# Two score matmuls on half the rows each: pairing the lower-part products of an attention tile on TensorE

## The chip, the core and the metric

One NeuronCore of one Trainium2 chip runs the whole program. The metric is the device time of one execution in microseconds (us): the median of several runs, and beside it the one execution that was taken with the hardware profiler, from which all rows come.

## What is computed

The program chains three blocks. The change is in the first, an attention with queries pooled by two:

```python
q_pool = q.reshape(B, H, S // 2, 2, D).mean(axis=3)      # B=2, H=8, S=1152, D=64
scores = scale * np.matmul(q_pool, k.transpose(0, 1, 3, 2))
scores = scores - np.max(scores, axis=-1, keepdims=True)
attn = np.exp(scores)
attn = attn / (np.sum(attn, axis=-1, keepdims=True) + 1e-09)
return np.matmul(attn, v)
```

The two blocks behind it are feed-forward layers: `x @ w_in`, a leaky ReLU, `@ w_out`; then four experts `relu(x @ w1[e]) @ w2[e]`, weighted by probabilities and added.

## The kernel before

**Two parts of every number.** Matmul operands are held as two parts, a higher one (`hi`, a copy into the matmul's type) and a lower one (`lo`, what is left over). A product is the sum of higher by higher, higher by lower and lower by higher.

**Pairs and tiles.** `pairs` lists 2 batches x 4 pairs of heads, `n` = 0 to 7. A pair has 9 tiles `t` of 128 query rows: `t` = 0 to 3 belong to its first head, 5 to 8 to its second, and `t` = 4 holds 64 rows of each. `tiles` lists all 72.

**Score operands.** `kst[n][h]`, called `K[h]`, has the head's keys on 128 partitions: the higher parts of the 64 dimensions on partitions 0 to 63, the lower parts on 64 to 127. `qst[n % 2][:, j, h]` has the queries, the same 64 dimensions on both halves of the partitions, with `j` = 1 for higher and `j` = 0 for lower parts (from pair 1 on). So one matmul with the higher parts of the queries gives two of the three products at once, and one with the lower parts gives the third (and the product of the two lower parts, which isn't needed). `kh_b[n % 2]`, called `k_hi_of[n]`, has the higher parts of both heads' keys: head 0 on partitions 0 to 63, head 1 on 64 to 127.

**The steps of one tile.** `emit_s` (L346) issues the scores, 1152 columns in three chunks of `CW` = 384, each in a PSUM bank of its own: per chunk a matmul with the queries' higher parts and one with their lower parts, so six matmuls a tile (nine for `t` = 4, of which three use `qmid`). VectorE (DVE) then moves the three banks to SBUF in one instruction and takes the minimum (L349); there is one set of three banks, so the next tile's scores wait for that. ScalarE (ACT) takes the exponential (L355), DVE adds 1e-9 and takes the reciprocal (L359, L363), GpSimd (POOL) normalises (L365). `emit_t` transposes the nine 128x128 blocks on TensorE (L386); ACT copies their higher parts (L390), DVE subtracts for the lower ones (L98, `tl`). `queue_av` lists the products with the values (L413) and `run_av` issues some of them in each tile.

**What sets the order.** The order is written out by hand: a loop over `tiles` emits, for tile `i`, the scores of tile `i + lead` (`lead` is 3 but for the first tiles), the transposes of tile `i`, some products with the values, the exponential of tile `i + lead`, and one step of the next pair's preparation from `prep_pair`. Its step `k_lo` has POOL take the keys' lower parts, and the SyncE (SP) queue copy higher and lower parts into `K[h]` (L282, L283); `q_lo` and its DMAs (L298) follow, and the loads of later pairs (L221, L222, L230). In the last pair DVE and ACT also prepare the first weights of the feed-forward block.

Of the kernel before, what the change touches and what calls it, by code (L numbers as in the profile page):

```python
# [27 lines left out]
CW = 384  # L28
# [5 lines left out]
def f32(ap):  # L34
    return ap.bitcast(F32)
# [3 lines left out]
def tile_kernel(ctx: ExitStack, tc: tile.TileContext, q, k, v, w_in, w_out, probs, w1, w2, out):  # L39
    nc = tc.nc  # L40
    PE, ACT, DVE, POOL, SP = nc.tensor, nc.scalar, nc.vector, nc.gpsimd, nc.sync

    def at(name, off, shape, dt=F32R):

        return nc.alloc_sbuf_tensor_at(name, [128, *shape], dt, offset=BASE + 4 * off).ap()
# [9 lines left out]
    qst = [at(f"qst{i}", 18432 + 2560 * i, [2, 2, SQ + 64]) for i in range(2)]  # L55
    qmid = [at(f"qmid{i}", 23552 + 128 * i, [128]) for i in range(2)]
    kh_b = [at(f"kh{i}", 23808 + 1152 * i, [S]) for i in range(2)]
    th_b = [at(f"th{i}", 26112 + 2880 * i, [NKB, 320]) for i in range(2)]
    tl_b = [at(f"tl{i}", 31872 + 2880 * i, [NKB, 320]) for i in range(3)]
    e_b = [at(f"e{i}", 41216 + 1152 * i, [S], F32) for i in range(5)]  # L60
# [28 lines left out]
    def hi(eng, dst, src):  # L89
        if eng is ACT:  # L90
            ACT.copy(dst, src)  # L91
        elif eng is POOL:
            POOL.tensor_scalar(dst, src, 1.0, 1.0, op0=ALU.mult, op1=ALU.mult)
        else:
            DVE.tensor_copy(dst, src)

    def lo(eng, dst, src, high):
        eng.tensor_tensor(dst, src, f32(high), op=ALU.subtract)  # L98
# [75 lines left out]
    def three_banks(i):  # L174
        return PS[:, 3 * i:3 * i + 3]
# [5 lines left out]
    def first_layer(f, src_h, src_l):  # L181
        ps = next_banks()
        wh, wl = a_t[f]

        def mms(k_, c):
            cs = slice(c * CW, (c + 1) * CW)
            PE.matmul(ps[:, c, :CW], wh[:, k_], src_h[:, k_, cs], start=k_ == 0, stop=False)  # L187
            PE.matmul(ps[:, c, :CW], wh[:, k_], src_l[:, k_, cs], start=False, stop=False)  # L188
            PE.matmul(ps[:, c, :CW], wl[:, k_], src_h[:, k_, cs], start=False, stop=k_ == KD - 1)  # L189
        return ps, mms  # L190


    with ExitStack() as actx:
# [15 lines left out]
        raw, raw_v, kst, vst, k_hi_of = {}, {}, {}, {}, {}  # L209

        def two_heads(n, name):
            return [kv[name, h, n % 2] for h in range(2)]

        def load_qk(n):
            if n >= len(pairs):
                load_a()
                load_a()
                return
            b, p = pairs[n]
            rk, rq = rk_b, rq_b.rearrange("p (a b) -> p a b", a=2)  # L220
            SP.dma_start(rk, k[b, p])  # L221
            SP.dma_start(rq, q[b, p])  # L222
            raw[n] = (rk, rq)

        def load_v(n):
            if n >= len(pairs):
                return
            b, p = pairs[n]
            raw_v[n] = rv_b.rearrange("p (a h d) -> p a h d", a=NKB, h=2)
            SP.dma_start(raw_v[n], v[b, p])  # L230
# [35 lines left out]
        def prep_pair(n):  # L266


            e_q, e_v = DVE if n == 1 else POOL, DVE if n == 0 else POOL
            rk, rq = raw.get(n, (None, None))  # L270

            def k_hi():
                kh = k_hi_of[n] = kh_b[n % 2]
                hi(ACT, kh, rk)

            def k_lo():
                kh = k_hi_of[n]
                ks = kst[n] = two_heads(n, "k")
                lo(POOL, rk.bitcast(F32R), rk, kh)
                for h in range(2):  # L280
                    r = slice(h * 64, h * 64 + 64)
                    SP.dma_start(f32(ks[h][0:64]), f32(kh[r]))  # L282
                    SP.dma_start(f32(ks[h][64:128]), rk[r])  # L283

            def q_add():
                POOL.tensor_tensor(rq[:, 0], rq[:, 0], rq[:, 1], op=ALU.add)

            def q_hi():
                hi(ACT, rq[:, 1].bitcast(F32R), rq[:, 0])

            def q_lo():
                lo(e_q, rq[:, 0].bitcast(F32R), rq[:, 0], rq[:, 1])
                t = qst[n % 2]
                for h in range(2):
                    r = slice(h * 64, h * 64 + 64)
                    hi(POOL, qmid[n % 2][r, r], rq[r, 0, (SQ - 64) * (1 - h):][:, :64])
                    for d in (slice(0, 64), slice(64, 128)):
                        SP.dma_start(f32(t[d, :, h, h * 64:h * 64 + SQ]), rq[r])  # L298

            def v_hi(h):  # L300
                if h == 0:
                    vst[n] = [t.rearrange("p (a b) -> p a b", a=NKB) for t in two_heads(n, "v")]
                a = h * 64
                hi(ACT, vst[n][h][:, :, a:a + 64], raw_v[n][:, :, h, :])

            def v_lo(h):
                a, c = h * 64, 64 - h * 64
                lo(e_v, vst[n][h][:, :, c:c + 64], raw_v[n][:, :, h, :], vst[n][h][:, :, a:a + 64])

            if n == 0:  # L310
                return [[lambda: v_hi(0)], [lambda: v_lo(0)], [lambda: v_hi(1)], [lambda: v_lo(1), lambda: load_v(1)]]
            return [[q_add, k_hi], [k_lo], [q_hi], [q_lo, lambda: load_qk(n + 1)], [lambda: v_hi(0)],
                    [lambda: v_lo(0), lambda: v_hi(1)], [lambda: v_lo(1), lambda: load_v(n + 1)]]
# [15 lines left out]
        def emit_s(i):  # L329
            n, t = tiles[i]  # L330
            ps = three_banks(0)
            Q, K = qst[n % 2], kst[n]
            if t < 4:
                use = [(0, t * 128)]
            elif t == 4:
                use = [(0, 512), (1, 0)]
            else:
                use = [(1, 128 + (t - 5) * 128)]
            for c in range(3):
                cs = slice(c * CW, (c + 1) * CW)  # L340
                mms = [(Q[:, j, h, c0:c0 + 128], K[h][:, cs]) for h, c0 in use for j in (1, 0)]
                if len(use) > 1 and n:

                    mms = mms[::2] + [(qmid[n % 2], k_hi_of[n][:, cs])]
                for m, (x, y) in enumerate(mms):
                    PE.matmul(ps[:, c, :CW], x, y, start=m == 0, stop=m == len(mms) - 1)  # L346
            e = e_b[i % 5].rearrange("p (a b) -> p a b", a=3)
            st = st_b[:, i % 6]
            DVE.tensor_scalar(e, ps[:, :, :CW], -0.5 / float(D) ** 0.5, None,  # L349
                              op0=ALU.mult, op1=ALU.min, accum_out=st[:, 0:1])  # L350
            s_sb[i] = (e, st)
# [89 lines left out]
        with tc.manual_schedule():  # L441
# [16 lines left out]
            at = dict.fromkeys(("s", "exp", "sum", "norm"), 0)  # L458

            def upto(what, emit, i):  # L460
                first = {"exp": "s", "sum": "exp", "norm": "sum"}
                while at[what] <= i and at[what] < (at[first[what]] if what in first else len(tiles)):
                    emit(at[what])
                    at[what] += 1

            upto("s", emit_s, 0)
            upto("exp", emit_exp, 0)
            q_lo(1)
            for c in range(3):
                k_hi(1, c)  # L470
            upto("s", emit_s, 1)
            upto("sum", emit_sum, 0)
            upto("norm", emit_norm, 0)
# [33 lines left out]
            for i, (n, t) in enumerate(tiles):  # L507
                if i in begin_at:
                    for d, fs in enumerate(prep_pair(begin_at[i])):
                        steps.setdefault(i + d, []).extend(fs)  # L510
                lead = 2 if i < L2 else 3
                upto("s", emit_s, i + lead)
                upto("sum", emit_sum, i + lead - 1)
                emit_t(i, lambda: upto("norm", emit_norm, i + lead - 1))
                run_av(AVB.get(t, AVD))
                if i == len(tiles) - 4:

                    f0_ps, mms = first_layer(0, xh, xl)
                    f0 = [(k_, c) for k_ in range(KD - 1) for c in range(NC)] + [(KD - 1, c) for c in range(NC)]
                if i >= len(tiles) - 4:  # L520
                    for _ in range(F0N[t - 5]):
                        mms(*f0.pop(0))
                upto("exp", emit_exp, i + lead)
                if t in (1, 4, 6, 8):
                    name, w = {1: ("A1", 256), 4: ("A2", 320), 6: ("B1", 320), 8: ("B2", 256)}[t]
                    queue_av(n, name, w, fast=n == len(pairs) - 1 and t > 4)
                for f in steps.get(i, []):
                    f()
                if n == len(pairs) - 1:
                    for f in ahead.get(t, []):  # L530
                        f()
# [207 lines left out]
    with tc.manual_schedule():  # L739
# [3 lines left out]
        ps, mms = first_layer(1, xh, xl)  # L743
# [8 lines left out]
        for f in range(2, n1):  # L752
            ps, mms = first_layer(f, xh, xl)
# [30 lines left out]
    with tc.manual_schedule():  # L784
# [24 lines left out]
        for what, *args in order:  # L809
            what(*args)  # L810
            if what is product:
# [5 lines left out]
                elif name == "P2" and p or name == "P7" and p == NPAIR - 1:  # L817


                    n = p - (name == "P2")  # L820
# [31 lines left out]
```

## Time and profile before

| | |
|---|---|
| median of 3 runs | 853.01 us (851.96 to 854.18) |
| the profiled execution | 852.96 us |
| its span, first to last instruction | 851.2 us |
| TensorE matmul (PE) busy | 824.2 us, 97% of the span |
| weight loads of TensorE (PEld) busy | 776.7 us, 91% |
| DVE / ACT / POOL busy | 574.0 / 435.4 / 412.6 us |
| mean granted TensorE clock | 0.990 |

The 1.8 us between the execution's time and its span lie before the first and behind the last instruction. Busy shares are means over stages that differ: attention fills the first 255 us or so, the feed-forward layers the rest. Matmuls are pipelined and the profile models their ends, so the duration of one matmul is longer than the distance from its start to that of the next.

### The profile page before, as it was taken

What the parts mean: (1) busy time and instruction counts of PE and PEld (TensorE: products, weight loads), DVE (VectorE), ACT (ScalarE), POOL (GpSimd) and SP (SyncE); (2) the same over time, 40 slices, a digit from 0 to 9 for tenths busy, and PEclk for the clock granted to TensorE, in tenths of its full rate; (3) what the DMA queues carried; (4) which work ended last, traced back from release to release, by engine and by line L of the source; (5) the groups of instructions that cost most, each with busy time, mean ns of one, the idle gap of its engine ahead of it and who ended that gap; (6) DMA issues with size and microseconds to landing.
All of it is one profiled execution on the core that took longest, in us unless ns stands there. A gap on an engine that the chain in (4) does not pass through costs nothing.

```text
span 851.2 us, 13547 instructions
## 1 busy us (share of the span) xinstructions
PE 824.2 (97%) x5071; PEld 776.7 (91%) x5071; DVE 574.0 (67%) x948; ACT 435.4 (51%) x763; POOL 412.6 (48%) x362
## 2 busy tenths in 40 slices
PE   6799999999989899999999999999999999999998
PEld 5689999999979799999999998989898998989886
DVE  5979999999997989777666772635445362726332
ACT  4878989999985665424422640505142342406030
POOL 1668888888862678565561060605133331504020
PEclk7999999999999999999999999999999999999999
DMA  7446446644701233322120020201111110201012
GB/s 195 111 127 181 106 132 169 157 105 131 197 5 63 85 111 111 99 71 78 51 99 25 26 99 1 99 1 53 47 50 50 49 51 1 99 1 50 0 38 99
DMA packets 25153, 68.65 MB, mean 81 GB/s; under 512 B 2944, under 2 KB 7040, under 8 KB 25088
## 3 DMA queue, kind: packets, MB, share of 16 engines
q1 hardware_dynamic: 25088, 67.79, 26.7%
q8 instruction: 40, 0.66, 0.3%
q14 instruction: 25, 0.20, 0.1%
HBM read 48.91 MB, written 2.36 MB: 60 GB/s over the span
## 4 chain that ended last, share of the span: by engine, by line
PE 82%; DVE 9%; issue 3%; DMA 2%; POOL 1%; ACT 1%; SPq 0%; POOLq 0%; DVEq 0%; ACTq 0%
PE ps L687 20%; PE ps L729 8%; PE ps L730 8%; PE ps L728 7%; PE ps L346 7%; PE ps L413 6%; PE ps L386 6%; PE ps L585 4%; PE ps L586 4%; PE ps L584 4%; DVE e L349 3%; PE ps L189 3%; PE ps L188 3%; PE ps L187 3%; DVE tl L98 2%
## 5 line engine op out<-in xcount | busy, mean ns | idle before, releaser
L98 POOL TENSOR_TENSOR bb<-w2r,bb 128x512 fp32r<-128x512 f32 x32 | 45.5, 1445 | 262.9 <-ACT bb L91 232.0
L735 DVE SCALAR_TENSOR_TENSOR oacc<-ps,pw,oacc 128x512 f32<-128x512 f32 x63 | 47.2, 749 | 101.4 <-PE ps L730 101.4
L365 POOL TENSOR_SCALAR e<-e,st 128x1152 f32<-128x1152 f32 x70 | 86.9, 1246 | 58.4 <-DVE st L363 42.4
L98 DVE TENSOR_TENSOR tl<-ps,th 128x384 fp32r<-128x384 f32 (+1 forms) x240 | 112.0, 503 | 1.9 <-ACT th L390 1.8
L729 PE MATMUL ps<-bb,gg 128*128 128x512 f32 x288 | 112.3, 390 | 0.9 <-POOL bb L98 0.8
L687 PE MATMUL ps<-yT,ws 128*128 128x288 f32 x768 | 111.5, 296 | 0.8 <-ACT cb L704 0.8
L728 PE MATMUL ps<-bb,gg 128*128 128x512 f32 x288 | 112.2, 390 | 0.0
L730 PE MATMUL ps<-bb,gg 128*128 128x512 f32 x288 | 112.1, 389 | 0.0
L349 DVE TENSOR_SCALAR_CACHE_REDUCE e<-ps 128x1152 f32<-128x1152 f32 x72 | 97.4, 1353 | 17.1 <-PE ps L346 16.1
L346 PE MATMUL ps<-k,qst 128*128 128x384 f32 x438 | 96.8, 353 | 11.8 <-DVE e L349 7.4
L687 PEld LDWEIGHTS ps<-yT,ws 128*128 128x128 f32 x768 | 105.7, 189 | 1.6 <-ACT cb L704 1.0
L390 ACT CAST th<-ps 128x384 fp32r<-128x384 f32 (+1 forms) x240 | 91.2, 458 | 25.1 <-PE ps L386 23.4
L693 ACT COPY ca<-ps 128x576 f32<-128x576 f32 x16 | 10.3, 641 | 167.6 <-PE ps L687 154.8
L355 ACT ACTIVATE e<-e,st 128x1152 f32<-128x1152 f32 x72 | 91.1, 1265 | 4.3 <-DVE e L349 2.6
L346 PEld LDWEIGHTS ps<-k,qst 128*128 128x128 f32 x438 | 77.0, 194 | 17.2 <-DVE e L349 11.7
L386 PE MATMUL ps<-ident,e 128*128 128x128 f32 x648 | 84.6, 276 | 4.9 <-POOL e L365 3.3
L386 PEld LDWEIGHTS ps<-ident,e 128*128 128x128 f32 x648 | 75.5, 142 | 10.6 <-POOL e L365 6.0
L687 PE MATMUL ps<-yB,ws 128*128 128x288 f32 x576 | 84.4, 296 | 0.0
L687 PEld LDWEIGHTS ps<-yB,ws 128*128 128x128 f32 x576 | 79.8, 189 | 0.5
L98 DVE TENSOR_TENSOR ws<-wf,ws 128x768 fp32r<-128x768 f32 (+1 forms) x32 | 41.5, 1298 | 46.3 <-ACT ws L91 46.3
L189 PE MATMUL ps<-xh,a 128*128 128x384 f32 x192 | 65.0, 339 | 2.8 <-POOL a L136 2.8
L187 PE MATMUL ps<-xh,a 128*128 128x384 f32 x192 | 64.9, 338 | 0.7 <-ACT gf L563 0.7
(126 smaller groups left out, 1723.7 us busy)
## 6 DMA issues: line engine op xcount, KB each, us to landing
wa<-in_w_in SPq DMA_DIRECT2D x16, 512.0 KB, 3.5
wb<-in_w_out SPq DMA_DIRECT2D x16, 512.0 KB, 4.2
wf<-in_w SPq DMA_DIRECT2D x32, 256.0 KB, 3.9
w2r<-in_w SPq DMA_DIRECT2D x16, 512.0 KB, 3.6
qst<-rq SPq DMA_DIRECT2D x28, 288.0 KB, 4.3
rv<-in_v SPq DMA_DIRECT2D x8, 576.0 KB, 5.5
rk<-in_k SPq DMA_DIRECT2D x7, 576.0 KB, 5.9
rq<-in_q SPq DMA_DIRECT2D x7, 576.0 KB, 4.8
```

The costliest lines, as they stand in the source:

```text
L98: eng.tensor_tensor(dst, src, f32(high), op=ALU.subtract)
L187: PE.matmul(ps[:, c, :CW], wh[:, k_], src_h[:, k_, cs], start=k_ == 0, stop=False)
L189: PE.matmul(ps[:, c, :CW], wl[:, k_], src_h[:, k_, cs], start=False, stop=k_ == KD - 1)
L346: PE.matmul(ps[:, c, :CW], x, y, start=m == 0, stop=m == len(mms) - 1)
L349: DVE.tensor_scalar(e, ps[:, :, :CW], -0.5 / float(D) ** 0.5, None, op0=ALU.mult, op1=ALU.min, accum_out=st[:, 0:1])
L355: ACT.activation(e, e, AF.Exp, bias=st[:, 0:1], scale=-1.0, accum_out=st[:, 1:2])
L386: PE.transpose(ps[:, j], e[:, (3 * g + j) * 128:(3 * g + j + 1) * 128], ident)
L390: ACT.copy(h, ps[:, :, s0:s0 + w])
L687: PE.matmul(ps[:, c, :HW], w[wi][:, i, ks], y[:, yi, k, c * HW:(c + 1) * HW], start=bool(first and k == 0 and m == 0), stop=k == 1 and m = ...
L728: PE.matmul(ps, gh[:, ts_], wh, start=f == fs[0], stop=False)
L729: PE.matmul(ps, gh[:, ts_], wl, start=False, stop=False)
L730: PE.matmul(ps, gl[:, ts_], wh, start=False, stop=f == fs[-1])
```

## The change

For every tile of pairs 1 to 7 but `t` = 4, the six score matmuls are written in another order and two of them on fewer rows. First come the three chunks with the queries' higher parts, on all 128 rows. Then chunk 2 with the lower parts, on 128 rows as before. Then chunk 0 with the lower parts on rows 0 to 63 alone (against the keys' higher parts there), and chunk 1 with the lower parts on rows 64 to 127 alone. For that the keys' higher parts of chunk 1 must lie on partitions 64 to 127. For the second head `k_hi_of[n]` has them there; for the first head one more DMA a pair copies 64 x 384 numbers into a new buffer `khs_b`. The product of the two lower parts is left out for chunks 0 and 1.

```diff
+    khs_b = [at(f"khs{i}", 51264 + CW * i, [CW]) for i in range(2)]
...
                     SP.dma_start(f32(ks[h][0:64]), f32(kh[r]))
                     SP.dma_start(f32(ks[h][64:128]), rk[r])
+                SP.dma_start(f32(khs_b[n % 2][64:128]), f32(kh[0:64, CW:2 * CW]))
...
-            for c in range(3):
+            if len(use) == 1 and n:
+                (h, c0), = use
+                hi_, lo_ = (Q[:, j, h, c0:c0 + 128] for j in (1, 0))
+                other = khs_b[n % 2] if h == 0 else k_hi_of[n][:, CW:2 * CW]
+                for c in range(3):
+                    PE.matmul(ps[:, c, :CW], hi_, K[h][:, c * CW:(c + 1) * CW], start=True, stop=False)
+                PE.matmul(ps[:, 2, :CW], lo_, K[h][:, 2 * CW:], start=False, stop=True)
+                PE.matmul(ps[:, 0, :CW], lo_[0:64], K[h][0:64, :CW], start=False, stop=True)
+                PE.matmul(ps[:, 1, :CW], lo_[64:128], other[64:128], start=False, stop=True)
+            for c in range(3) if len(use) > 1 or not n else ():
```

On TensorE's queue, at the first tiles of pair 1 (`k` is `K[0]`, `qst` the queries, `e` the normalised scores; 128x384 is what a matmul writes), there stood before:

```order
L346 MATMUL ps<-k_58,qst_66 128x384 x6
L386 MATMUL ps<-ident,e_77 128x128 x9
L413 MATMUL ps<-tl_74,v_61 128x320 x8
L346 MATMUL ps<-k_58,qst_66 128x384 x6
L386 MATMUL ps<-ident,e_78 128x128 x9
```

and now:

```order
L349 MATMUL ps<-k_58,qst_66 128x384 x3
L350 MATMUL ps<-k_58,qst_66 128x384
L351 MATMUL ps<-k_58,qst_66 128x384
L352 MATMUL ps<-khs_72,qst_66 128x384
L400 MATMUL ps<-ident,e_79 128x128 x9
L427 MATMUL ps<-tl_76,v_61 128x320 x8
L349 MATMUL ps<-k_58,qst_66 128x384 x3
L350 MATMUL ps<-k_58,qst_66 128x384
L351 MATMUL ps<-k_58,qst_66 128x384
L352 MATMUL ps<-khs_72,qst_66 128x384
L400 MATMUL ps<-ident,e_80 128x128 x9
```

The number of matmuls and their columns stay; the group is four matmuls on 128 rows, then the two on 64 rows (L351, L352), and the transposes come right behind these.

On SP's queue, at the preparation of pair 1 (`kh` the keys' higher parts of both heads, `rk` their lower parts), there stood before:

```order
L282 DMA k_58<-kh_70 64x1152
L283 DMA k_58<-rk 64x1152
L282 DMA k_60<-kh_70 64x1152
L283 DMA k_60<-rk 64x1152
L230 DMA rv<-in_v 128x1152
L298 DMA qst_66<-rq 64x2x576 x4
```

and now:

```order
L284 DMA k_58<-kh_70 64x1152
L285 DMA k_58<-rk 64x1152
L284 DMA k_60<-kh_70 64x1152
L285 DMA k_60<-rk 64x1152
L286 DMA khs_72<-kh_70 64x384
L232 DMA rv<-in_v 128x1152
L301 DMA qst_66<-rq 64x2x576 x4
```

One DMA is put between the copies of the keys and the next load of values; nothing else moves.

## Rows read from the trace of the kernel before

**Rows 1.** The page: engines (busy, share, instructions), then the span in 40 slices.

```profile
PE 824.2 (97%) x5071; PEld 776.7 (91%) x5071; DVE 574.0 (67%) x948; ACT 435.4 (51%) x763; POOL 412.6 (48%) x362
...
PE   6799999999989899999999999999999999999998
```

**Rows 2.** Busy time by stretch of 20 us, from 60 to 240 us, and their sum.

```profile
60.00:80.00 20.00, 19.34 (x141) 18.32 (x140) 18.56 (x49) 18.20 (x40) 18.89 (x20) 1.00 0.68 171
...
200.00:220.00 20.00, 19.90 (x149) 19.47 (x148) 19.20 (x50) 18.92 (x40) 17.72 (x18) 1.00 0.38 93
...
sum 180.00, PE 177.91 PEld 172.66 DVE 169.45 ACT 165.17 POOL 150.49; mean PE 19.77 PEld 19.18 DVE 18.83 ACT 18.35 POOL 16.72
```

**Rows 3.** The chain of waits over one pair: start us, us, what.

```profile
149.34 1.38 DVE e L349 x2
150.72 0.04 issue
150.76 1.31 PE ps L346 x6
152.07 0.98 PE ps L386 x9
153.06 1.19 PE ps L413 x10
154.25 1.05 PE ps L346 x6
...
173.60 1.07 PE ps L346 x6
...
178.50 1.36 DVE e L349
```

**Rows 4.** Groups of instructions from 149.3 to 178.5 us, the same pair.

```profile
L349 DVE TENSOR_SCALAR_CACHE_REDUCE e<-ps 128x1152 f32<-128x1152 f32 x9 | 12.2, 1353 | 1.4 <-PE ps L346 1.4
```

**Rows 5.** The chain of waits in the last pair: its tile `t` = 4, then the tail.

```profile
235.19 1.58 PE ps L346 x9
236.88 1.37 DVE e L349 x2
...
241.33 1.36 DVE e L349 x2
...
251.50 1.27 DVE e L349 x2
```

**Rows 6.** Line L346 alone in that pair: duration ns min/median/max.

```profile
L346 PEld LDWEIGHTS ps<-k,qst x54: 186/188/192, 150.8 to 177.7; 128*128 128x128 f32 x54
L346 PE MATMUL ps<-k,qst x54: 334/336/440, 150.8 to 177.9; 128*128 128x384 f32 x54
```

**Rows 7.** Timeline in mid tile, at 183.81 us: TensorE's matmuls, then its weight loads.

```profile
183.62 0.51 PE L346 MATMUL ps<-k,qst 128*128 128x384 f32 x2
...
183.62 0.36 PEld L346 LDWEIGHTS ps<-k,qst 128*128 128x128 f32 x2
```

**Rows 8.** Timeline at 179.9 us, a tile whose scores waited: matmul, then weight loads.

```profile
179.93 0.44 PE L346 MATMUL ps<-k,qst 128*128 128x384 f32 x1
...
179.92 0.30 PEld L346 LDWEIGHTS ps<-k,qst 128*128 128x128 f32 x2 [0.30 <-DVE e L349]
```

**Rows 9.** SP's queue over the preparation of pair 1, then its key copies' landing.

```profile
33.88 0.75 SPq L283 DMA_DIRECT2D k<-rk  x1
34.74 1.23 SPq L230 DMA_DIRECT2D rv<-in_v  x1
38.53 3.68 SPq L298 DMA_DIRECT2D qst<-rq  x4
...
k<-kh SPq DMA_DIRECT2D x14, 288.0 KB, 4.1
```

**Rows 10.** Waits ahead of the scores (us, times), then the chain at pair 1's start.

```profile
  DMA qst<-rq: 0.5, 1
...
43.02 0.60 issue
43.62 2.09 PE ps L346 x6
```

## The prediction

> **What bounds the kernel now.** I began with the page: PE is busy 97% of the span, and from the third slice on it shows 9 or 8 tenths throughout [rows 1]. That alone says little, since a matmul's duration is longer than its share of the queue. So I looked at the stage of the change by stretches of 20 us: between 60 and 240 us PE is busy 177.91 of 180 us, but DVE 169.45 (94%) and ACT 165.17 (92%) [rows 2]. The stage has little air anywhere. The chain of waits says who sets the pace: over one pair, from 149.34 to 178.50 us (29.16 us), it runs through scores (L346), transposes (L386) and products with the values (L413) tile after tile, and leaves TensorE once, for two evictions of DVE at the pair's start [rows 3]. DVE waits for scores 1.4 us in that pair [rows 4]. So TensorE paces, and DVE is about 5% behind it. In the last pair that turns round: its tile 4 is issued at 235.19 us, and from 236.88 us the chain goes through DVE [rows 5].
>
> The profiled execution (852.96 us) is within 0.05 us of the median of the runs (853.01), so what I add to or take from the one I add to the other. About 0.3% (2.6 us) is what a measurement of this kernel can tell from no change.
>
> **What the change touches.** Pairs 1 to 7 have 8 tiles each with `t` other than 4: 56 tiles. The scores of four of them (the last pair's 5 to 8) come after 235 us, in DVE's stretch [rows 5]; 52 are issued where TensorE paces.
>
> *A tile's scores before.* In mid tile two matmuls together take 0.51 us, one alone 0.336 [rows 6, 7], so they start 0.174 us apart; six of them are the 1.05 us of the chain [rows 3].
>
> *After.* Four matmuls on all rows keep their 0.174 each, 0.70. The trace has no matmul on half the rows (every form reads 128*128), so the last two are bounded by rows of full ones. At best the second costs nothing beside the first: 0.70 + 0.174 = 0.87, a gain of 0.174. What stands in the way is its weight load. A weight load starts together with the matmul ahead of it (both at 183.62) [rows 7], and where matmuls are short they follow each other at the pace of loads: nine transposes in 0.98, 0.109 each [rows 3]. If the second half's load starts only with the first half's matmul, the second starts 0.109 after the first: 0.70 + 0.109 + 0.174 = 0.98, a gain of 0.065. If both loads run under the fourth matmul, they need 0.218 of which 0.174 is covered, the pair starts 0.044 late, and the gain is 0.13. I take 0.10, the middle of 0.065 and 0.13: the two halves' weights lie in different rows, which speaks for the second, but no row shows a load that starts earlier than with the matmul ahead.
>
> 52 x 0.10 = 5.2 us less on TensorE. Per pair it is 0.8 of the 1.4 us that DVE now waits [rows 4], so DVE doesn't become the bound as a whole, but in single tiles it will: in the two at a pair's start it is on the chain already [rows 3]. I take a quarter off: 3.9 us. The four tiles in DVE's stretch give nothing.
>
> *The order of the six.* The three matmuls with higher parts now stand first. Each has its own weight load as before, and the eviction L349 waits for all three banks in either order. Cost nothing.
>
> *The added DMA.* It copies 64 x 384 numbers, 96 KB, seven times. SP reaches it after the keys' copies; an issue takes 0.5 to 0.75 us there, and behind it only the load of values is pushed back, since the DMAs of the queries start at 38.53, 2.6 us after that load's issue ended [rows 9]: SP waits there for something else, and this wait covers the issue. The data land some 4 us after issue [rows 9], near 39 us; pair 1's first scores start at 43.62 [rows 10], and later pairs have more room. One place is tight: those first scores waited 0.5 us for the queries' DMAs [rows 10]. 96 KB more in flight just ahead of them could cost a third of that, as it is a third of a 288 KB copy, so 0 to 0.5 us; I take 0.2. That is within what I rounded.
>
> *New readers.* `k_hi_of` is now read until a pair's last tile. Its next writer, the preparation of the pair after the next, starts in the loop's step of that same tile, whose scores were issued three steps earlier. The last pair's `khs_b` lies where raw weights are loaded at its tile 4, behind the scores of tiles 0 to 3. No wait is added where somebody would notice: nothing.
>
> Sum: 853.0 - 3.9 + 0.2 = 849.3 us.
>
> **Rival 1: the change of mode empties TensorE; slower.** Twice a tile the array goes from a matmul on 128 rows to one on 64 and back, at L351 and at the first transpose behind L352. Today such seams cost nothing: scores, transposes and values follow each other at 1.05, 0.98 and 1.19 us with no gap in the chain [rows 3], although the transposes are another kind of matmul. But no seam of today changes the rows. If TensorE had to run empty at such a seam, weight loads couldn't go ahead of it. What an exposed load costs shows where scores waited for DVE: load and matmul appear at 179.92 and 179.93, and the matmul takes 0.44 where 0.336 is usual [rows 6, 8], 0.10 more. Cheap end: the first half's load in the open (0.109), the second half's start 0.109 behind it, 0.174, and the first transpose's load in the open (0.109): 0.70 + 0.50 = 1.20, 0.15 more than before, and 52 x 0.15 = 7.8: 861 us. Dear end: besides, each seam waits for the end of the matmul ahead, 0.336 - 0.174 = 0.16 twice: 0.47 a tile, 24.7 us: 877 us. In the middle 869. TensorE has nothing to absorb it. The kernel becomes measurably slower from 0.05 us a tile on (2.6 / 52), that is when both seams together eat the 0.10 and half as much again. For it speaks that a new arrangement of the array is asked for 112 times; against it, that all other seams are free.
>
> The Trainium skill ("TensorEngine Tiling (Array Packing)", Key Properties) speaks for this rival: changing the tiling mode, it says, drains TensorE, while different tiles of one mode load and multiply in parallel. By that the sum would lie in this rival's range; the trace of before can't show it, because it has one mode only.
>
> **Rival 2: no difference.** Either the halves run one after the other (then there are six steps of 0.174 as before, 853 us), or the seams cost about 0.05 each, just what the overlap gives, or DVE, with 94% [rows 2], takes back the gain. All of these end within 2.6 us of 853.0, at 850.4 to 855.6. For it speaks how little air DVE and ACT have; against it, the 1.4 us a pair that DVE now waits for scores.
>
> **How the numbers follow.** Overlap without a cost at the seams: 0.45, of which 0.05 ends within 0.3% because DVE takes it back. Seams that cost more than the overlap: 0.38. No difference: 0.17. So faster 0.40, same 0.22, slower 0.38. I forecast the likeliest case, 849.3 us; its own range is 846 (0.13 a tile in full, 6.8 us) to 851 (0.065 less a third). The range of the whole goes from there up into Rival 1 until half of its 0.38 is left out, to its middle of 869: 846 to 869.
>
> **What would show it.** In the profile after, the two matmuls on half the rows (L351, L352) are a form of their own. Right: they start 0.04 to 0.11 us apart, the chain's score step falls from 1.05 to about 0.95, the first transpose starts 0.17 behind L352, and DVE's wait for scores falls below 1.4 us a pair. Rival 1: a gap of over 0.1 us ahead of L351, another ahead of the first transpose, with weight loads that don't overlap the matmul ahead, a score step of 1.2 or more, and DVE waiting more for scores. Rival 2: L352 starts 0.17 after L351, or the score step falls and waits on DVE (L349) grow ahead of it. My forecast is wrong if the score step isn't shorter than 1.05, or if it is and the pair still takes 29.16 us.

## The result and the profile after

The changed kernel takes 860.18 us (median of 4 runs, 859.87 to 861.21) against 852.86 us before (median of 4): 7.3 us slower, ratio 1.0089 with a 95% interval of 1.0075 to 1.0103. The profiled execution took 859.87 us, its span 858.0. The line numbers are now those of the changed kernel: L349 to L352 are the six score matmuls, L400 the transposes, L427 the products with the values, L363 the eviction by DVE.

The page after, engines, to be read against [rows 1]:

```profile
PE 832.3 (97%) x5071; PEld 763.6 (89%) x5071; DVE 574.7 (67%) x948; ACT 435.5 (51%) x763; POOL 412.3 (48%) x362
```

DVE, ACT and POOL work as long as before. TensorE is busy 8 us longer with the same 5071 matmuls, and its weight loads are busy 13 us less. The timeline of one tile shows how both come about.

A seam is a place where the number of rows changes; a tile has two. One tile's seams, from the timeline after at 158.6 us; first the matmuls, then the weight loads:

```profile
158.59 0.34 PE L350 MATMUL ps<-k,qst 128*128 128x384 f32 x1
158.86 0.44 PE L351 MATMUL ps<-k,qst 64*128 64x384 f32 x1
158.86 0.44 PE L352 MATMUL ps<-kh,qst 64*128 64x384 f32 x1
159.23 0.44 PE L400 MATMUL ps<-ident,e 128*128 128x128 f32 x2
```

```profile
158.42 0.19 PEld L350 LDWEIGHTS ps<-k,qst 128*128 128x128 f32 x1
158.86 0.18 PEld L351 LDWEIGHTS ps<-k,qst 64*128 64x128 f32 x1 [0.25 <-issue]
158.86 0.18 PEld L352 LDWEIGHTS ps<-kh,qst 64*128 64x128 f32 x1
159.23 0.31 PEld L400 LDWEIGHTS ps<-ident,e 128*128 128x128 f32 x3 [0.18 <-issue]
```

Here one sees the whole price of a tile. The two half matmuls are what the change promised: both loads and both matmuls start together at 158.86, so the second costs nothing. But the loads don't go under the last full matmul. That one starts at 158.59 and would make room after 0.174 us, at 158.77; the loads come at 158.86, 0.09 us later, after a gap that waits for nothing the profile shows ("issue"), and then the matmuls show 0.44 us where 0.336 is usual, 0.10 of exposed load. The way back is the same: the pair, under way from 158.96, would make room at 159.14, the transposes' first load comes at 159.23, and about 0.06 of it is exposed (the transposes take 1.13 us on the chain below where they took 0.98, less the gap of 0.09). That is 0.09 + 0.10 + 0.09 + 0.06, some 0.35 us for two seams, against 0.174 saved: a tile is 0.175 us longer.

The chain of waits after, over nine tiles from the eviction of one pair's tile 4 to that of the next, to be read against [rows 3]:

```profile
153.15 1.38 DVE e L363 x2
...
158.23 0.53 PE ps L349 x3
158.75 0.18 PE ps L350
158.93 0.37 PE ps L351
159.30 1.13 PE ps L400 x9
...
168.07 0.54 PE ps L349 x3
...
183.31 1.36 DVE e L363
```

Scores and transposes were 1.05 + 0.98 = 2.03 us a tile; they are 0.53 + 0.18 + 0.37 + 1.13 = 2.21. (The chain books the way back under the transposes.) The pair takes 183.31 - 153.15 = 30.16 us against 29.16, so 1.00 more, where eight tiles of 0.175 would make 1.40. The rest comes from the fifth scores in this stretch, those of the next pair's first tile. There, before, TensorE waited:

```profile
163.62 0.13 issue
163.75 1.28 PE ps L346 x6
```

These scores came late and with their load exposed, 0.13 + 1.28 against 1.05, a loss of 0.36 us. The profile names DVE as the releaser, but that work of DVE had ended at 163.30; the second of the four DMAs with that pair's queries, issued at 159.34, took 4.3 us and landed at 163.64, and the first load started at 163.72. After the change the same place (168.07) shows no wait: TensorE comes there later, and the queries have landed. So TensorE had 0.36 us of slack a pair which the seams could fill for nothing.

Where the difference arises along the program, from the timelines before and after: DVE's first eviction of pair 1, of pair 7, and the last of all.

```profile
45.84 1.36 DVE L349 TENSOR_SCALAR_CACHE_REDUCE e<-ps 128x1152 f32<-128x1152 f32 x1 [2.83 <-PE ps L346]
223.54 1.36 DVE L349 TENSOR_SCALAR_CACHE_REDUCE e<-ps 128x1152 f32<-128x1152 f32 x1 [0.41 <-PE ps L346]
251.43 1.34 DVE L349 TENSOR_SCALAR_CACHE_REDUCE e<-ps 128x1152 f32<-128x1152 f32 x1
```

```profile
47.39 1.36 DVE L363 TENSOR_SCALAR_CACHE_REDUCE e<-ps 128x1152 f32<-128x1152 f32 x1 [4.56 <-PE ps L352]
229.63 1.36 DVE L363 TENSOR_SCALAR_CACHE_REDUCE e<-ps 128x1152 f32<-128x1152 f32 x1 [0.39 <-PE ps L352]
258.01 1.34 DVE L363 TENSOR_SCALAR_CACHE_REDUCE e<-ps 128x1152 f32<-128x1152 f32 x1
```

Pair 1's first eviction is 1.55 us late; from there to pair 7's 4.54 are added, and 0.5 in the last pair. The 4.54 arise in pairs 2 to 6, 0.7 to 1.0 each; pair 1 takes as long as before from its first eviction to pair 2's (31.44 us against 31.47). So there are two losses, one at pair 1's start and one spread over the tiles behind pair 1. The first is there before any half matmul has run. The chain after, where pair 1's scores begin, against [rows 10]:

```profile
38.38 5.16 DMA qst<-rq
43.55 1.45 issue
44.99 1.30 PE ps L349 x3
```

The scores start at 44.99 instead of 43.62, 1.37 us late, and the chain comes out of the queries' DMA. The experiments take the two losses apart.

### The profile page after: what moved, and what is told of

The parts are those of the page before. It is cut to its first block, busy times and chain, and to the rows that moved or that the text cites. A ratio compares the mean times of both kernels' runs of the same rounds, so it can differ in the third digit from the quotient of the medians.

```text
span 858.0 us, 13560 instructions
## 1 busy us (share of the span) xinstructions
PE 832.3 (97%) x5071; PEld 763.6 (89%) x5071; DVE 574.7 (67%) x948; ACT 435.5 (51%) x763; POOL 412.3 (48%) x362
## 4 chain that ended last, share of the span: by engine, by line
PE 85%; DVE 7%; issue 2%; DMA 2%; ACT 1%; POOL 1%; SPq 0%; POOLq 0%; DVEq 0%; ACTq 0%
PE ps L701 20%; PE ps L743 7%; PE ps L744 7%; PE ps L742 7%; PE ps L400 7%; PE ps L427 7%; PE ps L598 4%; PE ps L600 4%; PE ps L599 4%; PE ps L349 3%; PE ps L191 3%; PE ps L190 3%; PE ps L189 3%; DVE e L363 3%; PE ps L351 2%
## 5 line engine op out<-in xcount | busy, mean ns | idle before, releaser
L363 DVE TENSOR_SCALAR_CACHE_REDUCE e<-ps 128x1152 f32<-128x1152 f32 x72 | 97.5, 1354 | 23.1 <-PE ps L352 13.2
L400 PE MATMUL ps<-ident,e 128*128 128x128 f32 x648 | 87.9, 281 | 4.3 <-POOL e L379 3.0
L400 PEld LDWEIGHTS ps<-ident,e 128*128 128x128 f32 x648 | 71.5, 142 | 17.9 <-issue 9.8
L743 PEld LDWEIGHTS ps<-bb,gg 128*128 128x128 f32 x288 | 54.0, 188 | 12.5 <-POOL bb L100 1.8
L190 PE MATMUL ps<-xl,a 128*128 128x384 f32 x192 | 64.9, 338 | 0.0
```

The source lines that it names most:

```text
L400: PE.transpose(ps[:, j], e[:, (3 * g + j) * 128:(3 * g + j + 1) * 128], ident)
L743: PE.matmul(ps, gh[:, ts_], wl, start=False, stop=False)
```

## The experiments

Theory A: every tile pays two changes of rows and gets one matmul back, and the DMA costs once, at pair 1's start. Rivals: the DMA carries it all (B), the order of the six matmuls does (C), or the pair itself is dear, two loads and two matmuls at once (D). Each kernel was timed against runs of the kernel before on the same chip.

**The copy alone.** The kernel before, plus

```diff
+    khs_b = [at(f"khs{i}", 51264 + CW * i, [CW]) for i in range(2)]
...
+                SP.dma_start(f32(khs_b[n % 2][64:128]), f32(kh[0:64, CW:2 * CW]))
```

> The kernel before, with the added copy of the keys' higher parts (seven DMAs of 96 KB) and nothing that reads it. In the trace of the change the first scores of pair 1 start at 44.99 us instead of 43.62. Theory A (seams: the two changes of rows a tile cost some 0.35 us, the side-by-side pair gives back 0.174, and the copy costs once, at pair 1's start): 853 + 1.4 = 854.3 us, with the delay of 1.4 us at pair 1's first scores and pairs of 29.2 us behind it. Rival B (the added DMAs carry the loss): 859 to 860 us, pairs of 30.2 us. Rival C (the order of the six matmuls carries it, and the later start too): 853 us.

Measured: 856.81 us, ratio 1.0052 (1.0037 to 1.0067): 4 us for seven copies that nobody reads, far more than expected. The chain at pair 1's start, then the stretches from 44 to 50 us (PE busy is the first number, the granted clock the third from the end):

```profile
41.03 5.03 DMA qst<-rq
46.06 0.01 issue
46.07 2.27 PE ps L348 x6
```

```profile
44.00:46.00 2.00, 0.00 (x0) 0.00 (x0) 0.00 (x0) 0.08 (x1) 0.00 (x0) 0.71 1.04 230
46.00:48.00 2.00, 1.93 (x6) 1.96 (x7) 0.00 (x0) 0.00 (x0) 0.00 (x0) 0.50 0.76 226
48.00:50.00 2.00, 2.00 (x12) 1.90 (x10) 1.54 (x4) 0.83 (x2) 0.00 (x0) 0.50 0.38 55
```

The same stretches before:

```profile
44.00:46.00 2.00, 2.00 (x9) 1.90 (x8) 0.16 (x1) 0.00 (x0) 0.00 (x0) 0.50 1.00 232
46.00:48.00 2.00, 2.00 (x13) 2.00 (x12) 2.00 (x6) 1.43 (x4) 0.00 (x0) 0.69 0.75 244
48.00:50.00 2.00, 2.00 (x15) 1.97 (x14) 0.86 (x3) 2.00 (x4) 2.00 (x2) 1.00 0.60 230
```

The DMA engines are full here (shares of 0.94 to 1.04 between 42 and 46 us before, in the change and in this run). The queries' DMAs are issued at the same time as before (38.55 against 38.53 us), but the second of them takes 6.6 us to land where it took 4.2 (5.7 in the change). Pair 1's scores start at 46.07 against 43.62. TensorE stands still until then, and the granted clock is at 0.50, the lower level of 1.2 GHz, until past 50 us; before, it was at 0.69 from 46 to 48 and at 1.00 after that. So 2.45 us of lateness become more. From pair 1's first eviction to pair 7's it takes 0.5 us longer than before (48.46 to 226.69 us in this profile), nothing like the 4.5 of the change, and all of it in pair 1: the five pairs behind it take 146.15 us together, before 146.23. So the six later copies cost nothing that shows. The place was as Theory A had it, the size was not.

**The order alone.** All six on 128 rows, no copy:

```diff
+                PE.matmul(ps[:, 2, :CW], lo_, K[h][:, 2 * CW:3 * CW], start=False, stop=True)
+                PE.matmul(ps[:, 0, :CW], lo_, K[h][:, 0 * CW:1 * CW], start=False, stop=True)
+                PE.matmul(ps[:, 1, :CW], lo_, K[h][:, 1 * CW:2 * CW], start=False, stop=True)
```

> The change's order (three matmuls with higher parts, then chunk 2, 0, 1 with lower parts), but all six on 128 rows, and no copy. Theory A: 853 us, score step 1.05 us. Rival B: 853 us. Rival C: 858 to 860 us.

Measured: 852.09 us, ratio 0.9998 (0.9989 to 1.0008). Rival C falls.

**Both halves on the same rows**, no copy; the edit is shown against the change:

```diff
-                PE.matmul(ps[:, 1, :CW], lo_[64:128], other[64:128], start=False, stop=True)
+                PE.matmul(ps[:, 1, :CW], lo_[0:64], K[h][0:64, 1 * CW:2 * CW], start=False, stop=True)
```

> As the change, but both half matmuls on rows 0 to 63 (chunk 1 takes its keys from there too), so not side by side, and no copy. Theory A: the two seams stay and nothing is given back: a tile is 0.35 us longer than before, the second half starts 0.17 us behind the first; 52 tiles x 0.35 = 18 us, less some 3 us of waits for DVE that vanish as they did in the change: 868 us (864 to 872). Rival D (the seam's price is the pair's own, two loads and two matmuls at once): no seam, 853 us. Rival B: 853 us.

Measured: 867.03 us, ratio 1.0168 (1.0153 to 1.0183). Lines L347 and L348, the two halves (duration ns min/median/max):

```profile
L347 PE MATMUL ps<-k,qst x56: 437/440/442, 44.4 to 264.3; 64*128 64x384 f32 x56
...
L348 PE MATMUL ps<-k,qst x56: 335/335/335, 44.7 to 264.6; 64*128 64x384 f32 x56
```

The first half has its load in the open (440), the second has it hidden again (335): the price is at the change of rows, not in a half matmul. Rival B falls, since without the copy the kernel is slower still, and so does Rival D.

**One half alone**, no copy: chunk 1 on 128 rows, chunk 0 last on rows 0 to 63.

```diff
+                PE.matmul(ps[:, 1, :CW], lo_, K[h][:, 1 * CW:2 * CW], start=False, stop=True)
+                PE.matmul(ps[:, 0, :CW], lo_[0:64], K[h][0:64, 0 * CW:1 * CW], start=False, stop=True)
```

> Three matmuls with higher parts, chunks 2 and 1 with lower parts on 128 rows, then chunk 0 alone on rows 0 to 63; no copy. Theory A: two seams, nothing given back, as with both halves on the same rows: 868 us (864 to 872), the gap ahead of the half matmul 0.27 us from the start of the matmul before, its load not ahead of it. If instead each half matmul costs by itself, this is half as bad as both halves on the same rows: 860 us. Rival B: 853 us.

Measured: 867.19 us, ratio 1.0171 (1.0154 to 1.0188). One half a tile costs as much as two: it is the seams that are paid.

**Four seams**, no copy: half, full, half.

```diff
+                PE.matmul(ps[:, 0, :CW], lo_[0:64], K[h][0:64, 0 * CW:1 * CW], start=False, stop=True)
+                PE.matmul(ps[:, 2, :CW], lo_, K[h][:, 2 * CW:3 * CW], start=False, stop=True)
+                PE.matmul(ps[:, 1, :CW], lo_[0:64], K[h][0:64, 1 * CW:2 * CW], start=False, stop=True)
```

> No copy; chunk 0 with lower parts on rows 0 to 63, then chunk 2 on 128 rows, then chunk 1 on rows 0 to 63: four changes of rows a tile and nothing side by side. Theory A: twice the seams of the kernel with both halves on the same rows, which was 14.3 us slower than before; the first 0.35 us a tile were partly covered by waits that went, the second are not: 52 x 0.35 = 18 us more, 885 us (882 to 889). If only the stretch of half rows as a whole has a price, whatever stands in it: 867 us.

Measured: 886.98 us, ratio 1.041 (1.0391 to 1.0429). Its chain, one tile:

```profile
153.05 0.52 PE ps L345 x3
153.57 0.37 PE ps L346
153.94 0.37 PE ps L347
154.31 0.36 PE ps L348
154.68 1.13 PE ps L396 x9
```

Each matmul behind a seam takes 0.36 or 0.37 on the chain where 0.174 is usual, full and half alike, and the transposes 1.13 where they took 0.98: four seams, 0.15 to 0.20 each.

**The pair twice**, in the change as it is:

```diff
+                PE.matmul(ps[:, 0, :CW], lo_[0:64], K[h][0:64, 0 * CW:1 * CW], start=False, stop=False)
+                PE.matmul(ps[:, 1, :CW], lo_[64:128], other[64:128], start=False, stop=False)
```

> The change in full, with the two half matmuls of a tile issued twice one after the other (the scores of chunks 0 and 1 get their lower-part product added twice). Theory A (the price is paid where the number of rows changes, twice a tile): one more step of 0.174 us a tile, weight loads within the half-row stretch hidden again, 52 x 0.174 = 9 us more than the change: 869 us (867.5 to 871). If each side-by-side pair pays for its own start (exposed loads and emptying, 0.35 us): 878 us.

Measured: 870.04 us, ratio 1.0205 (1.019 to 1.022), 10 us above the change; pairs take 31.56 us against 30.16, 0.175 a tile more. Within a stretch of half rows a further pair costs about one step of 0.174, loads included. So the two seams are a fixed price, which does not grow with the length of the stretch.

**The pair in the middle**: higher parts of chunks 0 and 1, the pair, then chunk 2's two matmuls.

```diff
+                PE.matmul(ps[:, 0, :CW], lo_[0:64], K[h][0:64, 0 * CW:1 * CW], start=False, stop=True)
                 PE.matmul(ps[:, 1, :CW], lo_[64:128], other[64:128], start=False, stop=True)
+                PE.matmul(ps[:, 2, :CW], hi_, K[h][:, 2 * CW:3 * CW], start=True, stop=False)
+                PE.matmul(ps[:, 2, :CW], lo_, K[h][:, 2 * CW:3 * CW], start=False, stop=True)
```

> The change in full with the pair put between full matmuls (higher parts of chunks 0 and 1, the pair, higher part of chunk 2, its lower part). Theory A: two seams a tile again, but the second leads into a matmul whose load is exposed as that of the pair's (0.105 us) and not into a transpose (0.06): 52 x 0.045 = 2.3 us more than the change, 862.5 us (861 to 864). If the seam's price lay in the transposes behind it: 853 to 856 us.

Measured: 864.84 us, ratio 1.0143 (1.0128 to 1.0159). That is 4.7 us more than the change, twice what was expected, and the median lies outside the expected range of 861 to 864. In the profile the seams give what they should: pairs take 30.55 us there against 30.16, 0.05 a tile. The profiled execution (863.07 us, the fastest of the four) also had pair 1's first eviction at 48.27 us, later than the change did (47.39). Why the median is higher still stays open.

**POOL copies instead of a DMA.**

```diff
-                SP.dma_start(f32(khs_b[n % 2][64:128]), f32(kh[0:64, CW:2 * CW]))
+                hi(POOL, khs_b[n % 2][64:128], f32(kh[0:64, CW:2 * CW]))
```

> The change in full, but the keys' higher parts are copied to the other partitions by POOL (64 x 384, one instruction a pair) and not by a DMA. It separates the seams from the copy. Theory A (both cost: the two seams of a tile by more than the overlap gives, and the DMA once, ahead of pair 1's first scores): pairs stay at 30.2 us against 29.2 before, pair 1's first scores start near 43.6 us as before, 858.5 us (857.5 to 859.5), so slower than before by 5 to 6.5 us. Rival B2 (the 4.1 us that the copy alone cost add up with the seams' part, which then is only 3.3): 856 us, pairs of 29.7. Rival E (the copy's cost comes only where TensorE would have been ahead anyway, so it vanishes beside the seams): 860 us.

Measured: 862.63 us, ratio 1.012 (1.0105 to 1.0135): worse than the DMA, and no rival's figure. The copy takes POOL 506 ns (median; 1.40 us in pair 1), and what POOL does behind it comes later. At pair 1 the queries' DMAs are issued at 39.90 us instead of 38.53, and the scores start at 45.07, late without any added DMA. Pairs 2 to 6 take 30.4 to 31.2 us against 30.16. In one of them the chain leaves TensorE for 6 us:

```profile
133.78 0.49 DVE e L363
134.27 0.79 issue
...
137.18 1.27 DVE e L363 x2
...
139.92 0.76 PE ps L349 x3
```

TensorE works through most of these 6 us; it stands still for 0.81, just ahead of 139.92, where the next pair's first scores wait: the second DMA with their queries, issued at about 134.8, takes 5.0 us to land. So this run doesn't separate the copy; it shows that POOL has no half microsecond free ahead of the queries either.

**The DMA behind the queries' DMAs**, in the change; the line is taken from its old place and put here:

```diff
                         SP.dma_start(f32(t[d, :, h, h * 64:h * 64 + SQ]), rq[r])
+                SP.dma_start(f32(khs_b[n % 2][64:128]), f32(k_hi_of[n][0:64, CW:2 * CW]))
```

> The change in full, its DMA issued behind the four DMAs of the queries instead of ahead of the load of values. Theory A: the queries land as before, the copy's data come about 1 us behind them, so the first tile of pair 1 waits for that in its last matmul: 859.5 us (858.5 to 860.5), pairs of 30.2 us. If the copy's place does not matter: 860.2 us. If the copy were hidden there: as with POOL's copy.

Measured: 877.29 us, ratio 1.03 (1.0271 to 1.033). None of the three expected figures came: the copy is late in every pair, not in the first alone. From the chain of a later pair:

```profile
110.72 4.26 DMA khs<-kh
114.98 0.04 issue
115.03 0.44 PE ps L352
115.46 1.66 PE ps L400 x9
```

The queries' own DMAs land only just in time (163.64 us for scores at 163.72 in the kernel before), and this copy comes behind them. TensorE has work for the first part of these 4.26 us and then stands still for 1.59, between the two halves of one tile; nine transposes then take 1.66 us instead of 1.13, with the granted clock at 0.73 from 115 to 117 us and 0.50 from 117 to 119.

**From pair 2 on.** The change, but pair 1's first head keeps six full matmuls, and pair 1 has no copy.

```diff
-                SP.dma_start(f32(khs_b[n % 2][64:128]), f32(kh[0:64, CW:2 * CW]))
+                if n > 1:
+                    SP.dma_start(f32(khs_b[n % 2][64:128]), f32(kh[0:64, CW:2 * CW]))
...
-            if len(use) == 1 and n:
+            if t > 4 and n or t < 4 and n > 1:
...
```

> The change in full but for the first head of pair 1, which keeps six matmuls on 128 rows, and pair 1 has no copy. Theory A (the copy costs only where the DMA engines are full, at pair 1's start, 1.4 us and what a slower clock adds there): pair 1's first eviction at 45.2 to 46.3 us as before, pairs of 30.2 us behind it, 858.3 us (857 to 859.2). If the copies cost in every pair: pairs stay at 30.2 too, but then POOL's or the DMA's place makes no difference and the time stays at 860.

Measured: 857.36 us, ratio 1.0055 (1.0039 to 1.007). First evictions of pair 1 and pair 7:

```profile
45.87 1.36 DVE L364 TENSOR_SCALAR_CACHE_REDUCE e<-ps 128x1152 f32<-128x1152 f32 x1 [2.76 <-PE ps L361]
228.15 1.36 DVE L364 TENSOR_SCALAR_CACHE_REDUCE e<-ps 128x1152 f32<-128x1152 f32 x1 [0.39 <-PE ps L353]
```

Pair 1 begins as before (45.84), and from there to pair 7 it takes 182.28 us, as in the change (182.24; before 177.70). So the copy of pair 1 carries 860.18 - 857.36 = 2.8 us (the two intervals together leave 1 to 4.7), and 4.9 us over the kernel before remain for the seams. The seams of four tiles went together with that copy; but pair 1 takes 31.49 us here against 31.44 in the change, so they cost nothing that shows.

**The second head alone.** The pair only in tiles 5 to 8, no copy of any kind.

```diff
-            if len(use) == 1 and n:
+            if t > 4 and n:
...
```

> The side-by-side pair only in tiles 5 to 8 of pairs 1 to 7, whose keys' higher parts lie on the right partitions already: no copy of any kind, 28 tiles (24 where TensorE paces) with two seams each. Theory A: 0.175 us a tile net, 24 x 0.175 = 4.2 us, of which waits for DVE that vanish take some back: 855.5 us (854.5 to 857.0), pairs 2 to 6 at 29.5 to 29.9 us. If the seams cost nothing net and the copy was all: 852.5 us.

Measured: 852.87 us, ratio 1.0009 (1.0000 to 1.0018): less than Theory A's range. Half the tiles with seams are almost free. Their pairs take 29.48 us, 0.3 more than before and not 0.7, because the wait ahead of the next pair's first tile (L357 here, on all rows) is gone:

```profile
161.26 1.13 PE ps L397 x9
162.39 1.31 PE ps L424 x9
163.70 1.07 PE ps L357 x6
```

I had subtracted that wait too late: the first 0.36 us a pair are paid by slack, whatever the number of tiles. Four tiles cost 4 x 0.175 - 0.36 = 0.34 a pair, eight 1.40 - 0.36 = 1.04, and both are what the profiles show (0.3 and 1.0). Over pairs 2 to 6 that is 1.3 us. The whole kernel lost less because pair 1 was 0.75 us shorter in this profile than before (30.72 against 31.47); it was as short with the order alone (30.79), where there are no seams, so that part is no gain of the change.

**Values after queries.** The kernel before, with pair 1's load of values behind the queries' DMAs and its steps two tiles later, in the hope of a version that beats both:

```diff
-                return [[lambda: v_hi(0)], [lambda: v_lo(0)], [lambda: v_hi(1)], [lambda: v_lo(1), lambda: load_v(1)]]
+                return [[lambda: v_hi(0)], [lambda: v_lo(0)], [lambda: v_hi(1)], [lambda: v_lo(1)]]
+            if n == 1:
+                return [[q_add, k_hi], [k_lo], [q_hi], [q_lo, lambda: load_v(1), lambda: load_qk(2)], [], [],
+                        [lambda: v_hi(0)], [lambda: v_lo(0), lambda: v_hi(1)], [lambda: v_lo(1), lambda: load_v(2)]]
```

> The kernel before (no half rows, no copy), with pair 1's load of values issued behind its queries' DMAs, not ahead of them, and its steps on the values two tiles later. Theory A says that pair 1's first scores wait for the queries because the DMA engines are full ahead of them. Then 576 KB less ahead of them let those scores start up to 2 us earlier (at 41.5 to 43 us against 43.62), TensorE's clock need not fall there, and the kernel gains 1 to 3 us: 851 us (849.5 to 852.0). If something else is late there (the evictions, the values): 852.7 us or more.

Measured: 852.47 us, ratio 1.0005 (0.9996 to 1.0015). The expected gain did not come. The chain names the previous tile's eviction ahead of pair 1's first scores, and they start at 44.16:

```profile
42.08 1.38 DVE e L352 x2
43.46 0.71 issue
44.16 1.29 PE ps L349 x6
```

But that eviction had ended 0.7 us earlier. The second of the queries' DMAs, issued at 39.7, takes 4.3 us and lands at 44.0: the scores still wait for the queries, and these land no faster without the 576 KB of values ahead of them (4.2 us before). So the part of Theory A that explained the copy's price by what stands ahead in full DMA engines doesn't hold as it was put: 576 KB ahead cost the queries nothing that shows, and 96 KB more cost them 1.5 us in the change. What the traces show beside that: the copy's issue takes SP 1.30 us, so the values are issued at 35.95 instead of 34.74 and land at 42.3 instead of 41.6, and the queries land behind them. Whether it is this shift or the copy's own transfer that makes them late is not shown. No version that was tried is faster than the kernel before.

## Why the prediction was wrong

I forecast 849.3 us and the change took 860.2: inside the range, but slower where I had forecast faster, beside the cheap end of Rival 1.

- **The seams.** This is the step that failed. The sum of the likeliest case has no term for them: I priced them at nothing because "today such seams cost nothing" [rows 3], and gave the case that they cost more than the overlap 0.38. But those rows show a change of the kind of matmul, not of rows, as the prediction itself says. Seven kernels show an average price of 0.17 to 0.20 us for each change of rows: with one half, two in a row, two side by side, that pair twice, or halves apart (worked out from the time of a pair, 31.52 us with one half, 31.50 with two in a row, 34.52 with four seams, against 29.17 and the 0.36 of slack). Two a tile are 0.35 us, twice what the overlap gives back. The Trainium skill's rule ("TensorEngine Tiling (Array Packing)", Key Properties), that changing the tiling mode drains TensorE, agrees with this trace: gaps of 0.09 us with nothing issued, and no weight load ahead of the matmul before. By the prediction's own sign (wrong if the score step isn't shorter than 1.05 us) the forecast fails too: the step is 0.53 + 0.18 + 0.37 = 1.08.
- **What bounds the kernel** held in the main: TensorE paces the pairs, and what its tiles lose goes to the end, less what waits take up. But I took the chain's one exit to DVE [rows 3] for two evictions at a pair's start. It is one, with the short read of its minimum, behind the nine matmuls of tile 4. The wait at a pair's real start, 0.36 us for its queries, I did not see.
- **The overlap** was better than my middle: I took 0.10 between 0.065 and 0.13, and the halves start together, so it is 0.174, the end I had called the best. That the second load would wait for the first half's matmul was wrong. The Trainium skill's statement ("TensorEngine Tiling (Array Packing)", Key Properties) that tiles of one mode load and multiply in parallel agrees with both loads at 158.86.
- **The added DMA.** I gave it 0 to 0.5 us and took 0.2. In the change it costs 2.8 us, alone 4. I had counted its bytes as a share of a copy beside it, and its issue as 0.5 to 0.75 us, where it takes 1.30. The queries behind it are awaited, so pair 1 starts 1.37 us late, and TensorE's granted clock is at 0.50 for some microseconds there; before, it is at 0.50 for a shorter time, which the rows by stretch around 44 us would have shown. Why 96 KB delay the queries so much stays open.
- **DVE.** I took a quarter off a gain. There was no gain; and the slack that did count was not DVE's but the wait for the queries, which took 0.36 us a pair off the loss. So Rival 1's "TensorE has nothing to absorb it" was wrong too.
- **The order and the new readers** cost nothing, as forecast. With the order alone the ratio is 0.9998. The new readers do add one wait: in the last pair SP holds a load of raw weights for 9.0 us until L352 has read `khs_b`, and issues it at 239.68 us instead of 225.01. Nothing that shows hangs on it: from the last eviction to the end it takes 600.0 us against 599.8.
- **Rival 1's sum.** Its cheap end, 861 us, is near the result by luck, as a sum of other terms: 0.15 a tile over 52 tiles with nothing absorbed was 7.8 us; the seams made 4.9 and the copy 2.8. Its form was wrong in two places: the second half's load is not behind the first's, and each seam also has a gap of 0.09 us, where I had put 0 or 0.16.

## What to carry to other kernels

Putting two half matmuls side by side saves one step, but a stretch of half rows pays for its entry and exit: here 0.35 us, two steps of 384 columns. One pair in every tile can't earn that. By the same numbers it would take a stretch of more than two pairs, collected without a return to full rows in between; no run here tried that.

A copy is not priced by its bytes but by who is behind it: here 96 KB cost 2.8 us in pair 1 and nothing that shows in the six pairs after it. Look at how long its issue takes, and at what waits for the transfers after it. And before one calls an engine saturated, one should look for its regular waits, which absorb the first part of any loss.

## What was not expected of the hardware

- The two half matmuls are fully concurrent: both loads and both matmuls start within the 0.01 us that the timeline shows, and a second pair costs one step.
- A weight load across a change of rows is not hidden, one within a stretch of half rows is (440 ns for the half matmul behind full ones, 335 for the half matmul behind another half).
- A copy of 96 KB ahead of awaited transfers cost 2.8 to 4 us, with the granted clock at 0.50 for some microseconds after TensorE had stood still. 576 KB ahead of the same transfers cost nothing that shows (852.47 us without them there, 852.43 with them).
- 0.5 us more of POOL once a pair made the kernel some 2.5 us slower than the DMA did (862.63 us against 860.18).
